# Where in a slot VectorE's side work is issued: an attention and FFN kernel on one core

## Chip, core and metric

The kernel runs on one core of one Trainium2 chip. The metric is the device time of one execution in microseconds (us). The kernel before takes 370.85 us, the median of three runs (370.76 to 371.12). One more execution was recorded with the hardware profiler, and all rows of the profile come from that one.

## What is computed

The inputs are q, k and v with 8 batches, 8 heads, 576 positions and 64 features, s with one value per batch, head and position, and the three weight matrices and the norm vector of an FFN. All are float32.

```python
scores = scale * np.matmul(q, k.transpose(0, 1, 3, 2))
cum = np.cumsum(np.maximum(s, 0.0), axis=-1)
bias = -(cum[:, :, :, None] - cum[:, :, None, :])
scores = np.where(causal, -1e9, scores + np.minimum(bias, 0.0))
attn = softmax(scores)                   # with 1e-9 in the denominator
x = (attn @ v), heads side by side       # 4608 tokens of 512
xn = x / sqrt(mean(x * x) + 1e-6) * rms_g
out = (silu(xn @ w_gate) * (xn @ w_val)) @ w_out
```

## The kernel before

**Two kinds of work in one stream.** The FFN is cut into nine chunks of 512 tokens (chunk 0 starts at 30.9 us, chunk 1 at 72, chunk 2 at 111, chunk 3 at 150, chunk 4 at 190, chunk 5 at 227). The attention of batch 0 runs ahead of chunk 0; that of later batches is threaded through the chunks. A function `ffn` writes a chunk's matmuls: twelve pairs of gate (L670, with wg_sb) and value matmuls (L679, with wv_sb) of four each, and then the out-projection (L692), four blocks of twelve. Their results lie in four PSUM buffers, psF, taken in turn. ScalarE makes a tanh T of the gate (L673), VectorE the product U (L682) and then Ht (L675, L687); U frees the gate's buffer, Ht the other. ScalarE copies a block of the out-projection from its psF to osb (L697), and SyncE sends it out (L699).

**Slots.** Between these matmuls, 36 times per chunk, `ffn` calls `step`. A call is a slot: it writes a few pieces of attention into the engines' queues. Nothing is rescheduled afterwards (the kernel asks for a manual schedule), so the order in which `step` writes is the order in which every engine works. In a slot come, in this order:

1. What is left of the score step begun in the slot before: the second half of its exponentials on ScalarE (L274), and on GpSimd the causal mask over them (L283).
2. x_scale (L338), if a token block's values are three slots old: VectorE multiplies the block by its norm factor al_all and the norm vector. SyncE's transposing DMA (L348, L350) then brings the block into xnT, from which the FFN chunks read.
3. One piece from each of several queues of side work: loads on ScalarE (`act_side`), transposing DMAs for keys and queries (L171), loads of v and k (`v_side`, `pool_side`) and casts on GpSimd.
4. One piece from `dve_side`, VectorE's side work.
5. Either a score step or up to two of: a transposition of the norm's output (`do_xt`), a value step (`do_av`), a transposition of keys or queries (`do_t`). With a score step of batch 1, a `do_t` may come as well.

**Side work of VectorE.** `dve_side` holds two casts of batch 1's Q (L141), and for every batch's keys and queries a range check: `check_mag` strips the signs into mag (L369, 128 x 2560), and two calls of `check_max` take a running maximum into acc (L375, 128 x 1280 each). Nobody reads acc before the end of the kernel. From the third batch on, the checks are issued in the last slots of a chunk, during the out-projection. The end of the kernel adds a few small steps for a range test.

**A score step** (`do_s`, L250) multiplies keys with queries on TensorE into the one score buffer, psS. Four or eight exponentials (L274) read it, half of them in the slot itself, half at the head of the next. The next score step waits until they are done.

**A value step** (`do_av`, L300 and L306) multiplies the exponentials with v for four heads. The result goes to one of two PSUM buffers, psAV for the first half of the heads and psT for the second. VectorE forms a reciprocal of the sums (L313) and multiplies (L315) into x_sb; the text calls this pair the values. Behind the second half, ScalarE squares x_sb with a running sum (L321, the Square), GpSimd makes the norm factor from it (L328, L331), and x_scale of a later slot uses that.

These are the lines in question in the value step:

```python
nc.vector.reciprocal(out=rZ[0:n], in_=pv[0:n, :, 64])
...
nc.vector.tensor_tensor(
    out=xo[:, g * 256:(g + 1) * 256].rearrange("p (h d) -> p h d", h=4),
    in0=pv[0:n, :, 0:64], in1=rZ[0:n].unsqueeze(2).to_broadcast([n, 4, 64]), op=ALU.mult)
```

The slot itself and what calls it:

Of the kernel before, what the change touches and what calls it, by code (L numbers as in the profile page):

```python
# [26 lines left out]
def kernel(  # L27
# [131 lines left out]
    def kq_dma(b, w, c):  # L159

        if w == 0:
            n = rows(c)
            src = kqn[0:n, b % 2, 0, c].rearrange("p h d -> p (h d)")
            dst = kqTx[:, b % 2, 0, c, :, 0:n]
        elif c < 4:
            src = kqn[32 * c:32 * c + 32, b % 2, w, 0:4].rearrange("p r h d -> p (r h d)")
            dst = kqTx[:, b % 2, w, c].rearrange("d h (r p) -> d (h r) p", r=4)
        else:
            src = kqn[0:64, b % 2, w, 4].rearrange("p h d -> p (h d)")
            dst = kqTx[:, b % 2, w, 4, :, 0:64]  # L170
        nc.sync.dma_start_transpose(out=dst, in_=src)  # L171
# [50 lines left out]
    def slot_free():  # L222
        return eread.get(ecount[0] % NE, 0) == 0
# [111 lines left out]
    def x_scale(b, qb):  # L335
        n = rows(qb)
        col = b * NSC + qb
        nc.vector.scalar_tensor_tensor(  # L338
            out=xs_sb[0:n, (b * NSC + qb) % NX, :], in0=x_sb[0:n, (b * NSC + qb) % NX, :],
            scalar=al_all[0:n, col:col + 1], in1=g_row[0:n], op0=ALU.mult, op1=ALU.mult)  # L340

    def xt_dma(b, qb):

        n = rows(qb)
        t0 = (b * S + qb * 128) % RING
        m = min(n, RING - t0)
        i = (b * NSC + qb) % NX
        nc.sync.dma_start_transpose(out=xnT[:, :, t0:t0 + m], in_=xs_sb[0:m, i, :])  # L348
        if m < n:
            nc.sync.dma_start_transpose(out=xnT[:, :, 0:n - m], in_=xs_sb[m:n, i, :])  # L350
# [46 lines left out]
    def at(*key):  # L397
        return done.get(key, 10 ** 6)

    def ready(lag, *key):  # L400
        return at(*key) + lag <= slot[0]

    def run_side(queue):
        if queue and queue[0][0]():
            queue.pop(0)[1]()
            return True
        return False
# [21 lines left out]
    def phase():  # L429

        return slot[0] - first[0]
# [14 lines left out]
    def casts(b):  # L446

        def key(c):  # L450
            load_k(b, c)
            done["K", b, c] = slot[0]
            if c == NSC - 1:
                check(b)

        def over(w):
            done["cast", b, w] = slot[0]
            if b + 1 < B and (w == 1 or b + 1 < KB):
                loads(b + 1, w, early, 4)
            if w == 1:  # L460
                x_seq.extend((b, ww, c) for c in range(NSC) for ww in ((1, 0) if b >= KB else (1,)))
            else:
                done["cast", b] = slot[0]
                check(b)

        def free(w):
            return ready(0, "check", b - 2, w) and (
                ready(0, "T", b - 2) if w == 0 and b < KB + 2 else
                b < XB + 2 or ready(4, "X", b - 2, w, 4))
        if b >= KB:  # L470
            pool_side.extend((lambda: free(0) and slot[0] % 2 == 0, lambda c=c: key(c)) for c in range(NSC))
        fns = [(1, lambda r=r: cast_x(nc.gpsimd, b, 1, r)) for r in range(NSC)]
        fns += [(1, lambda: over(1))]
        if b < KB:
            fns += [(0, lambda r=r: cast(nc.gpsimd, b, 0, r, r + 1)) for r in range(NSC)]
            fns += [(0, lambda: over(0))]
        pool_side.extend((lambda w=w: ready(7, "raw", b, w) and free(w), f) for w, f in fns)
# [11 lines left out]
    def do_t(key, **kw):  # L489
        b, hp, w = key  # L490
        if hp == "tail":
            tail_step(b)
            done["T", b] = slot[0]
            after_tail(b)
        else:
            if b == 1:
                kw["dve"] = w == 1 and hp > 1
                if hp % 2:
                    kw["pT"] = psF16()
            t_step(b, hp, w, **kw)  # L500
        done["T", b, hp, w] = slot[0]
        last["T"] = slot[0]

    def do_s(key, pair=None):
        b, kb, g = key
        second = s_step(b, kb, g, pair)
        done["S", b, kb, g] = slot[0]
        if kb == 4:
            done["S", b, 4, 1] = slot[0]
        last["S"] = slot[0]  # L510
        return second
# [18 lines left out]
    def can_t():  # L530
        if not t_seq:
            return False
        b, hp, w = t_seq[0]
        if b >= XB and at(*(("XT", 1, 3) if b == 2 else ("AV", b - 1, (2, 1, 0, 0, 0)[b - 3], 1))) > slot[0]:
            return False
        if b >= XB and av_seq[0][2] == 1 and can_av(True):
            return False
        if slot[0] - last["T"] < (1 if b < XB else 2 if b < 4 else 3) or slot[0] - last["AVT"] < 3:
            return False
        return (ready(2, "cast", b) or ready(2, "cast", b, w)) and (b < 2 or ready(1, "S", b - 2, 4, 0))  # L540

    def can_s():
        if not s_seq or not slot_free():
            return False
        b, kb, g = s_seq[0]
        if b == 1 and (phase() < 24 and phase() % 2 == 0 or kb == 4 and at("AV", 1, 3, 1) > slot[0]):
            return False
        due = SLOTS * ((b * S + kb * 128) // DM) - (26 if b == 1 else 18 if b < 4 else 14)
        if slot[0] - last["S"] < (4 if slot[0] < due - 24 else 3 if slot[0] < due else 2):
            return False  # L550
        if b >= XB:
            return all(ready(5, "X", b, 1, c) for c in (kb, min(kb + 1, 4))) and (
                ready(5, "X", b, 0, kb) if b >= KB else ready(3, "T", b) if kb >= 3 else
                all(ready(3, "T", b, hp, 0) for hp in (2 * g, 2 * g + 1)))
        if kb >= 3 and not ready(3, "T", b):
            return False
        if kb == 4:
            return True
        return all(ready(3, "T", b, 2 * g + j, w) for j in (0, 1) for w in (0, 1))
# [18 lines left out]
    def by_pe(b, qb):  # L578

        return b == 0 or (b, qb) == (1, 3)  # L580

    def can_xt():
        if not xt_seq or slot[0] - last["T"] < 2:
            return False
        b, qb = xt_seq[0]
        if (b, qb) == (0, 4) and at("T", 1) > slot[0]:
            return False
        return ready(4 if b else 6, "AV", b, qb, 1) and by_pe(b, qb)
# [10 lines left out]
    def step(bare=False):  # L599

        slot[0] += 1
        while pending:
            pending.pop(0)()
        moved = False
        if scaled[0] < len(x_list):
            b, qb = x_list[scaled[0]]
            if ready(3, "AV", b, qb, 1):
                x_scale(b, qb)
                scaled[0] += 1
                if not by_pe(b, qb):  # L610
                    assert xt_seq[0] == (b, qb)
                    xt_dma(*xt_seq.pop(0))
                    done["XT", b, qb] = slot[0] + 4
                    moved = True
        run_side(act_side)

        if not moved and x_seq and slot[0] - last["X"] >= 2 and not (
                scaled[0] < len(x_list) and ready(1, "AV", *x_list[scaled[0]], 1)):
            b, w, c = x_seq[0]
            if (ready(2, "cast", b, 1) and ready(1, "S", b - 2, 4, 0)  # L620
                    and (w == 1 or ready(7, "K", b, c))):
                x_seq.pop(0)
                kq_dma(b, w, c)
                done["X", b, w, c] = last["X"] = slot[0]
                if b >= KB and (w, c) == (0, NSC - 1) and b + 2 < B:
                    casts(b + 2)
        bare = bare or chunk[0] == 0 and 30 <= phase() <= 33
        if slot[0] % 2 and not bare and not (chunk[0] == 0 and phase() >= 24):
            run_side(v_side)
        if not bare:  # L630
            run_side(pool_side)
        run_side(dve_side)
        if can_s():
            pending.append(do_s(s_seq.pop(0)))
            if t_seq and t_seq[0][0] == 1 and can_t():
                do_t(t_seq.pop(0))
            return
        n = 0
        if can_xt():
            do_xt(xt_seq.pop(0))  # L640
            n += 1
        if can_av():
            do_av(av_seq.pop(0))
            n += 1
        if n < 2 and t_seq and can_t():
            do_t(t_seq.pop(0))
# [466 lines left out]
```

## Time and profile before

| | us |
|---|---|
| median of three runs | 370.85 (370.76 to 371.12) |
| the profiled execution | 371.13 |
| its span, first to last instruction | 369.5 |
| TensorE (PE) busy in it | 346.3 |
| VectorE (DVE) busy | 277.1 |
| ScalarE (ACT) busy | 238.4 |
| GpSimd (POOL) busy | 176.1 |
| mean granted TensorE clock | 0.998 |

TensorE's busy time by stage: 19.55 of the 30.9 us ahead of chunk 0, 116.84 of the 119.1 us of chunks 0 to 2, 38.08 of the 40 us from 150 to 190 (chunk 3), 109.21 of the 110 us from 190 to 300, and 62.66 of the last 69.5 us.

How to read the profile: a row of a timeline gives start, length, engine, source line, what is written from what, and in brackets the engine's idle time in front with what ended it. "[0.96 <-ACT E L274]" says that the engine had nothing to do for 0.96 us, until ScalarE's line 274 had written E. Rows that follow each other on one engine overlap by some 0.08 us, because an instruction starts while the one before it drains. PEld is the loading of weights, which runs beside the matmuls. An average share of busy time says little here: what counts is whether TensorE waits, and for whom, in a given stage.

### The profile page before, as it was taken

The page shows a single profiled execution, that of the slowest core. Times are in us where ns is not written, and L with a number is a line of the kernel's source. Part 1 is how long each engine was busy: PE and PEld are TensorE (multiplying, and loading weights), DVE is VectorE, ACT ScalarE, POOL GpSimd, SP SyncE. Part 2 cuts the span into 40 slices and gives each one's busy share as a digit, 9 for nine tenths or more (in the row PEclk, how much of TensorE's full clock was granted, in tenths as well). Part 3 has the DMA queues.
Part 4 walks back from the last instruction along what each step waited for, and adds up shares of the span by engine and source line. Part 5 has one row for each costly group of instructions (what it writes and reads, how often), then busy time and mean ns, then how long its engine had stood idle before and what let it go on. Part 6 is the DMA issues. An engine that isn't in the chain of part 4 may idle for free.

```text
span 369.5 us, 6891 instructions
## 1 busy us (share of the span) xinstructions
PE 346.3 (94%) x2312; PEld 162.7 (44%) x2356; DVE 277.1 (75%) x523; ACT 238.4 (64%) x624; POOL 176.1 (48%) x281
## 2 busy tenths in 40 slices
PE   1888999999999999899999999999999999999992
PEld 1554544444444444444444444444444444444441
DVE  6777989599887878789989889885488558827820
ACT  3977686557896688677678766776677644223311
POOL 4968637948648375779637933632222200000000
PEclk9999999999999999999999999999999999999999
DMA  8999999999969299949969964992300230020011
GB/s 233 172 231 244 165 221 220 157 206 201 181 131 122 44 200 150 170 92 181 146 171 189 167 97 129 107 96 51 106 17 14 44 106 3 0 85 30 0 60 63
DMA packets 125627, 46.23 MB, mean 125 GB/s; under 512 B 104912, under 2 KB 120784, under 8 KB 125584
## 3 DMA queue, kind: packets, MB, share of 16 engines
q0 software_dynamic: 59920, 11.80, 45.5%
q1 hardware_dynamic: 53040, 24.33, 33.4%
q10 hardware_dynamic: 12624, 9.59, 10.6%
q8 instruction: 20, 0.33, 0.4%
q14 instruction: 23, 0.19, 0.2%
HBM read 38.16 MB, written 9.44 MB: 129 GB/s over the span
## 4 chain that ended last, share of the span: by engine, by line
PE 69%; DVE 9%; POOL 7%; issue 5%; DMA 5%; ACT 4%; ACTq 0%; SPq 0%; POOLq 0%; DVEq 0%
PE psF L692 22%; PE psF L670 19%; PE psF L679 19%; PE psS L250 4%; DMA kq<-in_q_dram 3%; ACT E L274 2%; POOL v_sb L175 2%; DVE acc L375 2%; DVE U L682 2%; DVE Ht L675 2%; POOL E L283 2%; DMA kq<-in_k_dram 2%; DVE x_sb L315 1%; POOL kqn L141 1%; PE psT L306 1%
## 5 line engine op out<-in xcount | busy, mean ns | idle before, releaser
L274 ACT ACTIVATE E<-psS,biasK 128x256 bf16<-128x256 f32 (+3 forms) x352 | 114.9, 415 | 19.2 <-PE psS L250 17.8
L670 PE MATMUL psF<-xnT,wg_sb 128*128 128x512 bf16 x426 | 110.2, 379 | 1.3 <-ACT xnT L364 0.7
L679 PE MATMUL psF<-xnT,wv_sb 128*128 128x512 bf16 x408 | 109.3, 379 | 1.3
L692 PE MATMUL psF<-wout_sb,Ht 128*128 128x512 bf16 x419 | 100.5, 379 | 0.5 <-issue 0.2
L682 DVE SCALAR_TENSOR_TENSOR U<-T,psF 128x512 bf16<-128x512 f32 x108 | 73.7, 682 | 29.0 <-ACT T L673 28.9
L283 POOL TENSOR_SCALAR_AFFINE_SELECT E<-E 128x512 bf16<-128x512 bf16 x72 | 52.2, 726 | 83.9 <-ACT E L274 83.5
L673 ACT ACTIVATE T<-psF 128x512 f32<-128x512 f32 x108 | 64.5, 597 | 42.1 <-PE psF L670 36.7
L675 DVE TENSOR_TENSOR Ht<-U,psF 128x512 bf16<-128x512 bf16 x99 | 67.7, 684 | 6.6
L670 PEld LDWEIGHTS <-wg_sb 128*128 128x128 bf16 x432 | 38.8, 98 | 45.7 <-issue 6.6
L679 PEld LDWEIGHTS <-wv_sb 128*128 128x128 bf16 x432 | 38.6, 98 | 42.5 <-issue 4.4
L692 PEld LDWEIGHTS <-Ht 128*128 128x128 bf16 x432 | 38.7, 98 | 42.0 <-issue 2.3
L338 DVE SCALAR_TENSOR_TENSOR xs_sb<-x_sb,al_all,g_row 128x512 bf16<-128x512 bf16 (+1 forms) x40 | 32.1, 804 | 15.0 <-POOL al_all L331 15.0
L697 ACT ACTIVATE osb<-psF 128x512 f32<-128x512 f32 x36 | 21.4, 595 | 31.8 <-PE psF L692 29.0
L321 ACT ACTIVATE xs_sb<-x_sb 128x512 bf16<-128x512 bf16 (+1 forms) x36 | 22.9, 639 | 22.8 <-DVE x_sb L315 22.5
L175 POOL DMA_DIRECT2D v_sb<-in_v_dram x40 | 35.0, 874 | 0.3 <-issue 0.2
L375 DVE TENSOR_TENSOR acc<-acc,mag 128x1280 bf16<-128x1280 bf16 x32 | 29.0, 921 | 0.4
L250 PE MATMUL psS<-kqT 64*128 64x256 bf16 (+2 forms) x304 | 26.8, 262 | 2.6 <-ACT E L274 2.0
L306 PEld LDWEIGHTS <-E 128*128 128x128 bf16 x320 | 23.1, 101 | 11.4 <-POOL E L283 0.8
L328 POOL TENSOR_SCALAR al_all<-ss_all 128x1 f32<-128x1 f32 (+1 forms) x40 | 12.6, 316 | 28.2 <-ACT xs_sb L321 23.7
L300 PEld LDWEIGHTS <-E 128*128 128x128 bf16 x256 | 21.2, 101 | 8.1 <-DVE x_sb L315 0.7
L331 POOL TENSOR_TENSOR al_all<-al_all,mhalf 128x1 f32<-128x1 f32 (+1 forms) x40 | 22.2, 555 | 3.3
L250 PEld LDWEIGHTS <-kqT 64*128 64x128 bf16 x320 | 10.4, 97 | 30.5 <-issue 29.2
(94 smaller groups left out, 280.4 us busy)
## 6 DMA issues: line engine op xcount, KB each, us to landing
out_dram<-osb SPq DMA_DIRECT2D x36, 256.0 KB, 2.2
kq<-in_q_dram ACTq DMA_DIRECT2D x6, 1024.0 KB, 7.8
v_sb<-in_v_dram POOLq DMA_DIRECT2D x32, 128.0 KB, 7.6
kq<-in_k_dram ACTq DMA_DIRECT2D x2, 1024.0 KB, 11.0
kqn<-in_k_dram POOLq DMA_DIRECT2D x16, 128.0 KB, 4.7
wg_sb<-in_moe_w_gate_dram POOLq DMA_DIRECT2D x2, 768.0 KB, 9.4
wv_sb<-in_moe_w_val_dram POOLq DMA_DIRECT2D x2, 768.0 KB, 12.0
wout_sb<-in_moe_w_out_dram POOLq DMA_DIRECT2D x1, 1536.0 KB, 15.0
```

What stands on the lines that cost most here:

```text
L175: nc.gpsimd.dma_start(out=v_sb[0:n, b % 2, c, :, 0:64], in_=v[b, :, c * 128:c * 128 + n, :].rearrange("h p d -> p h d"))
L250: nc.tensor.matmul(pair[par][:, j * W:j * W + M], lhsT=kT, rhs=qT, start=(j == 0), stop=(j == nj - 1))
L274: nc.scalar.activation(out=eo, in_=ei, func=AF.Exp, scale=0.125, bias=biasK[:, kb, bh:bh + 1])
L283: nc.gpsimd.affine_select(out=Ev[:, :, 0:nq], in_=Ev[:, :, 0:nq], pattern=[[0, nh], [1, nq]], compare_op=ALU.is_ge, fill=0.0, base=0, chan ...
L338: nc.vector.scalar_tensor_tensor(out=xs_sb[0:n, (b * NSC + qb) % NX, :], in0=x_sb[0:n, (b * NSC + qb) % NX, :], scalar=al_all[0:n, col:col ...
L375: nc.vector.tensor_tensor(out=acc[:, sl], in0=acc[:, sl], in1=mag[:, sl], op=ALU.max)
L670: nc.tensor.matmul(Gp, lhsT=wg_sb[:, cc, fs], rhs=xnT[:, cc, x0:x0 + DM], start=(cc == 0), stop=(cc == CC - 1))
L673: nc.scalar.activation(out=T, in_=Gp, func=AF.Tanh, scale=0.5)
L675: nc.vector.tensor_tensor(out=Ht[:, fb - 1, :], in0=pend[0], in1=pend[1], op=ALU.mult)
L679: nc.tensor.matmul(Vp, lhsT=wv_sb[:, cc, fs], rhs=xnT[:, cc, x0:x0 + DM], start=(cc == 0), stop=(cc == CC - 1))
L682: nc.vector.scalar_tensor_tensor(out=U, in0=T, scalar=1.0, in1=Gp, op0=ALU.add, op1=ALU.mult)
L692: nc.tensor.matmul(Op, lhsT=Ht[:, fb, tb * 128:(tb + 1) * 128], rhs=wout_sb[:, fb, :], start=(fb == 0), stop=(fb == FB - 1))
```

## The change

The body of the slot behind the call for `dve_side` becomes a function of its own, `place`, and is called ahead of it. So steps 4 and 5 of the list above trade places: in a slot that has both, VectorE gets the instructions of the score, value or transposition step first, and the piece of side work behind them. Which slot a piece falls into doesn't change.

```diff
@@ in step
             run_side(v_side)
         if not bare:
             run_side(pool_side)
+        place()
         run_side(dve_side)
+
+    def place():
+
         if can_s():
             pending.append(do_s(s_seq.pop(0)))
             if t_seq and t_seq[0][0] == 1 and can_t():
```

## The prediction

> **What bounds the kernel.** The busy times come first. TensorE is busy 346.3 of 369.5 us, so the other engines matter only where they make it wait.
>
> ```profile
> PE 346.3 (94%) x2312; PEld 162.7 (44%) x2356; DVE 277.1 (75%) x523; ACT 238.4 (64%) x624; POOL 176.1 (48%) x281
> ```
>
> Next, TensorE's waits. Most of its idle time is the lead-in before the first FFN chunk at 30.9 us and the tail, which the change leaves alone. Behind that, only one group has a size: scores (L250) that wait for ScalarE's exponentials.
>
> ```profile
> PE psS L250 <- ACT E L274: 2.0, 4, 1.0
> ```
>
> TensorE's timeline gives the places. The two largest are the second score step of chunk 3 and the last score step behind that chunk's out-projection. Both wait for the one score buffer (psS), which is free once four exponentials have read it.
>
> ```profile
> 154.08 0.39 PE L250 MATMUL psS<-kqT 64*128 64x256 bf16 x4 [0.96 <-ACT E L274]
> 189.34 0.39 PE L250 MATMUL psS<-kqT 64*128 64x256 bf16 x4 [0.58 <-ACT E L274]
> ```
>
> Why are the exponentials late? ScalarE's timeline: each time a Square (L321) heads its queue and has idled 2.0 and 2.5 us for VectorE's values (x_sb, L315). Behind the Square stand an output copy (L697) and the exponentials, with nothing between them.
>
> ```profile
> 150.88 0.63 ACT L321 ACTIVATE xs_sb<-x_sb 128x512 bf16<-128x512 bf16 x1 [2.00 <-DVE x_sb L315]
> 151.51 0.58 ACT L697 ACTIVATE osb<-psF 128x512 f32<-128x512 f32 x1
> ...
> 153.17 0.86 ACT L274 ACTIVATE E<-psS,biasK 128x256 bf16<-128x256 f32 x2
> ...
> 186.62 0.63 ACT L321 ACTIVATE xs_sb<-x_sb 128x512 bf16<-128x512 bf16 x1 [2.50 <-DVE x_sb L315]
> ```
>
> And why are the values late? VectorE's timeline, two short windows for the first place and a longer one for the second: the reciprocal (L313) that opens the values stands right behind range-check maxima (L375).
>
> ```profile
> 148.28 0.83 DVE L375 TENSOR_TENSOR acc<-acc,mag 128x1280 bf16<-128x1280 bf16 x1
> ...
> 149.02 1.27 DVE L375 TENSOR_TENSOR acc<-acc,mag 128x1280 bf16<-128x1280 bf16 x1
> 150.22 0.17 DVE L313 RECIPROCAL rZ<-psT 128x4 f32<-128x4 f32 x1
> ...
> 184.89 1.15 DVE L375 TENSOR_TENSOR acc<-acc,mag 128x1280 bf16<-128x1280 bf16 x1
> 185.96 0.17 DVE L313 RECIPROCAL rZ<-psT 128x4 f32<-128x4 f32 x1
> ```
>
> The products that these reciprocals read were finished long before: TensorE's last value matmul starts at 148.72 (0.19 long) and at 182.72.
>
> **What moves.** Set side by side, the two programs have the same instructions; the order differs on VectorE only. ScalarE, GpSimd, SyncE with all its DMAs, and TensorE keep theirs. Eleven of VectorE's side instructions trade places: one maximum with a key/query copy in chunk 0, nine maxima and one mask (L369) with a pair of reciprocal and product. The two casts of batch 1's Q don't move: no values stand in their slots. Nothing is added or removed, so the sum is one of waits.
>
> **Does a moved reciprocal block the queue?** It is VectorE's only new risk of waiting, since the maximum would then be stuck behind it. At each place I compared the time at which VectorE would reach the reciprocal with the end of its matmuls: 101.0 against 100.7, 139.5 against 139.2, 149.05 against 148.9, 181.6 against 178.9, 184.9 against 182.9, 189.8 against 187.0, 218.1 against 218.15, 223.1 against 222.3, 224.4 against 224.3, 226.6 against 226.5. At most 0.1 us each: cost 0. In chunk 0 the copy at 45.33 could go at 44.60 and its transposes ended at 43.5; TensorE has no gap there until 53.55 (0.34, behind exponentials of a later score step): 0.
>
> **First place (154.08).** The second maximum goes behind the values, so the reciprocal starts at about 149.05 instead of 150.22: 1.17 earlier. Bounds: 0.8, if the maximum were as short as its neighbour (0.83), and 1.17; I take 1.15, the row itself. The Square goes from 150.88 to 149.73, the copy to 150.36 (its matmuls end at 148.75 + 1.03 = 149.78, so it isn't held), the exponentials to 150.83 (scores ready at 149.71 + 0.39 = 150.10), the tanh to 151.55 (gate matmuls end at 151.15), the last exponentials end at 154.03 - 1.15 = 152.88. TensorE finishes the gate matmuls in front at 152.09 + 1.03 = 153.12. So TensorE, not psS, is late next: the whole 0.96 goes, with 0.24 to spare. **-0.96** (with the short maximum: -0.7).
>
> **Second place (189.34).** Before, the reciprocal of 185.96 stood behind two maxima of this stage, two masks, a pair of values and the third maximum (1.15). After, that third maximum stands behind it: 185.96 - 184.89 = 1.07 earlier. The Square goes to 185.55, the copy to 186.18 (its matmuls end at 182.75 + 2.75 = 185.50), the four exponentials end at 189.29 - 1.07 = 188.22; TensorE is done with the out-projection at 186.87 + 1.89 = 188.76. The 0.58 goes whole, with 0.5 to spare. The chain of waits names matmuls as what released the copy at 187.25; but it starts as the Square's accumulator read does elsewhere (0.09 behind it, no idle time), so I put it down to the Square. If the chain is right, this place gives 0. **-0.58**
>
> **The other places** give the engine behind them time that TensorE doesn't wait for: no gap over 0.17 us stands between 190 us and the end. **0**
>
> **What could be given back.** (a) At 139.56 the maximum now stands in front of x_scale (L338, 141.12): 139.53 + 0.55 of values + 0.75 = 140.85, still before it. But this x_scale leads, through the next values, Square and x_scale at 145.47, to a transposing DMA issued at 146.25; with 3.8 us, the median landing of that stretch, it lands at 150.05, and chunk 3's first matmul is at 150.13. Whatever delays it by over 0.1 us, TensorE pays. The nearest rows are a maximum of 0.83 (gain of up to 0.26, hidden) and one of 1.27 (x_scale 0.2 late). I take 0.1, and keep 0 and 0.2.
>
> A rule bears on this: the Trainium skill, "SBUF — State Buffer", section "Who interferes with whom", says that a VectorE instruction with two SBUF inputs and a GpSimd instruction that reads SBUF exclude each other, and that the one issued first holds the shared port to its end. This trace agrees: GpSimd's 0.19 us row L328 took 0.79 at 139.65, beside a maximum begun 0.09 earlier, and the maximum of 149.02 took 1.27 with a GpSimd select at 148.96 to 149.62. By that rule the moved maximum would stand behind GpSimd's L331, which would run from about 139.9 to 140.5, and end at 141.25; the sum would have 0.13 here in place of 0.1.
>
> (b) The FFN stage runs close: its four psF buffers are freed by VectorE, and at 174.60 the gate matmuls start 0.05 behind the product that freed theirs, at 207.44 the same. TensorE keeps its gain only if VectorE is as much earlier. It is: 1.15 against 0.96, then 1.15 + 1.07 against 1.54. Cost 0; if VectorE kept only 1.15 by 207, TensorE would lose 0.4.
>
> **Sum.** -0.96 - 0.58 + 0.1 = -1.44 us. The profiled execution took 371.13 us, 1.63 outside its span of 369.5; this one would have 368.1 and 369.7. It is 0.28 above the median of 370.85, so I forecast **369.4** as a median (0.39% less).
>
> **Rivals.**
> - Only one place closes. The first alone: 370.85 - 0.96 + 0.1 = 370.0, if the chain of waits is right about 187.25. The second alone: 370.3 to 370.4, if x_scale's lateness (0.2) and a short maximum take the first. For it: both margins rest on starts 0.2 to 0.5 us apart. Against: the links are in-order queues without idle time.
> - Nothing is kept: 370.85. Chunks 3 and 4 are tied to VectorE by (b), and an earlier TensorE only meets later buffers there. For it: DVE is busy 17.03 of the 19.5 us from 154.5 to 174. Against: its idle time there ends with ScalarE's tanh, which comes earlier too.
> - Slower: maxima meet GpSimd. At chunk 4's head two maxima stand together in front of the last values and the first U (L682, 192.69); before they took 1.13 and 0.81. The longest maximum of the trace took 2.27 (86.16, beside two GpSimd casts). Two such cost 4.54 - 1.94 = 2.60 more. The third gate matmuls' weights load 0.54 after that U frees their buffer, so TensorE pays from 0.54 on: 2.06. With the first place gained and the second not, +1.1: 371.95. Against: the median maximum is 0.82, and GpSimd has no cast from 182.1 to 196.
>
> **Chances.** Forecast 0.50; first place alone 0.13, second alone 0.07; nothing 0.17; slower 0.13. About 0.2% (0.74 us) is what a measurement of this kernel can tell from no change. Faster by more: 0.50 + 0.13 = 0.63; within it: 0.07 + 0.17 = 0.24; slower: 0.13. The forecast's own range is 369.0 (TensorE's 0.15 gap at 177.28, before another score step, goes too, and nothing is given back) to 369.8 (0.4 lost by 207). With the single places and with nothing kept it reaches to 370.9, which leaves out the slower case.
>
> **What would show it.** Right: no wait before the scores that stood at 154.08 and 189.34; the Squares' idle times of 2.00 and 2.50 down by about 1.1 each; chunk 3 starting within 0.1 us of 150.1. Wrong: a wait at the same scores with a later Square; a gap before chunk 3's first gate matmul; TensorE waiting for U or Ht at 170 to 210; maxima of over 1.2 us in the new places.

## The result and the profile after

| | before | after |
|---|---|---|
| median, run in turn on one chip, 7 runs each | 370.76 us (369.7 to 371.24) | 368.74 us (368.38 to 370.21) |
| ratio, 95% interval | | 0.9957 (0.9938 to 0.9976) |
| the profiled execution | 371.13 us, span 369.5 | 370.21 us, span 368.6 |

The changed kernel is faster by 0.43% (0.24 to 0.62%), or 1.6 us of 370.76 (0.9 to 2.3). That is the ratio of the means; the medians alone lie 2.0 us apart. The busy times hardly differ, as they should with the same instructions. Of the waits for scores a quarter is left, in chunks 0 and 1. From the page of the changed kernel and its list of waits (total us, number, longest):

```profile
PE 345.4 (94%) x2312; PEld 161.6 (44%) x2356; DVE 278.7 (76%) x523; ACT 239.0 (65%) x624; POOL 174.1 (47%) x281
...
PE psS L250 <- ACT E L274: 0.5, 2, 0.3
```

TensorE's timeline after, at the two places that waited 0.96 and 0.58. There is no bracket any more, so no idle time in front:

```profile
154.39 0.39 PE L250 MATMUL psS<-kqT 64*128 64x256 bf16 x4
188.99 0.39 PE L250 MATMUL psS<-kqT 64*128 64x256 bf16 x4
```

ScalarE's timeline after: the two Squares, whose idle time was 2.00 and 2.50 and is now 0.74 and 0.84.

```profile
150.81 0.63 ACT L321 ACTIVATE xs_sb<-x_sb 128x512 bf16<-128x512 bf16 x1 [0.74 <-DVE x_sb L315]
185.25 0.63 ACT L321 ACTIVATE xs_sb<-x_sb 128x512 bf16<-128x512 bf16 x1 [0.84 <-DVE x_sb L315]
```

VectorE's timeline after, first place: the reciprocal now stands between the two maxima, and idles 0.26 for its matmuls. The second maximum takes 0.82, not 1.27.

```profile
149.05 0.83 DVE L375 TENSOR_TENSOR acc<-acc,mag 128x1280 bf16<-128x1280 bf16 x1
150.14 0.18 DVE L313 RECIPROCAL rZ<-psT 128x4 f32<-128x4 f32 x1 [0.26 <-PE psT L306]
...
150.70 0.82 DVE L375 TENSOR_TENSOR acc<-acc,mag 128x1280 bf16<-128x1280 bf16 x1
```

So two executions can be compared, I measure each chunk from the first weight load of its first gate matmul to that of the next chunk (us):

| profile | to chunk 0 | chunk 0 | 1 | 2 | 3 | 4 |
|---|---|---|---|---|---|---|
| before | 30.00 | 42.12 | 38.99 | 38.98 | 39.56 | 37.36 |
| before, a second profile | 29.84 | 41.54 | 39.00 | 39.21 | 38.89 | 37.37 |
| after | 30.07 | 43.20 | 39.00 | 39.15 | 37.88 | 37.36 |
| after, a second profile | 29.73 | 41.51 | 39.80 | 39.14 | 37.88 | 37.35 |

From chunk 5 on all four agree within 0.01 us, up to the tail. The gain is in chunks 2 and 3: 78.54 and 78.10 before, 77.03 and 77.02 after. Chunks 0 and 1 vary by 1.7 and 0.8 us with the same program, and the tail by 0.6, which is why one profiled execution of the changed kernel is only 0.92 us below that of before. In it chunk 0 met a stretch at half clock (columns: window, length, busy time of PE, PEld, DVE, ACT and POOL, granted clock, DMA share, GB/s):

```profile
31.10:34.50 3.40, 3.18 (x8) 1.22 (x8) 3.40 (x3) 1.64 (x3) 3.19 (x5) 0.50 1.23 241
```

The granted clock is 0.50 for 3.41 us there, and 1.00 in the same stretch of the other three. The comparison below therefore uses chunks 2 and 3 of each profile beside the timed ratio.

### The profile page after: what moved, and what is told of

The parts are those of the page before. It is cut to its first block, busy times and chain, and to the rows that moved or that the text cites. A ratio compares the mean times of both kernels' runs of the same rounds, so it can differ in the third digit from the quotient of the medians.

```text
span 368.6 us, 6892 instructions
## 1 busy us (share of the span) xinstructions
PE 345.4 (94%) x2312; PEld 161.6 (44%) x2356; DVE 278.7 (76%) x523; ACT 239.0 (65%) x624; POOL 174.1 (47%) x281
## 4 chain that ended last, share of the span: by engine, by line
PE 78%; POOL 7%; issue 5%; DVE 4%; ACT 3%; DMA 2%; ACTq 0%; POOLq 0%; DVEq 0%
PE psF L696 25%; PE psF L674 21%; PE psF L683 21%; PE psS L250 5%; ACT E L274 2%; POOL E L283 2%; POOL v_sb L175 2%; DMA kq<-in_k_dram 2%; POOL kqn L141 1%; PE psT L306 1%; PE psAV L306 1%; PE psAV L300 1%; PE psT L300 1%; POOL al_all L331 1%; DVE Ht L679 1%
## 5 line engine op out<-in xcount | busy, mean ns | idle before, releaser
L283 POOL TENSOR_SCALAR_AFFINE_SELECT E<-E 128x512 bf16<-128x512 bf16 x72 | 50.9, 707 | 93.1 <-ACT E L274 92.7
L338 DVE SCALAR_TENSOR_TENSOR xs_sb<-x_sb,al_all,g_row 128x512 bf16<-128x512 bf16 (+1 forms) x40 | 32.1, 803 | 13.9 <-POOL al_all L331 13.9
L321 ACT ACTIVATE xs_sb<-x_sb 128x512 bf16<-128x512 bf16 (+1 forms) x36 | 23.0, 640 | 16.2 <-DVE x_sb L315 16.1
L306 PEld LDWEIGHTS <-E 128*128 128x128 bf16 x320 | 22.4, 99 | 12.2 <-POOL E L283 1.9
L331 POOL TENSOR_TENSOR al_all<-al_all,mhalf 128x1 f32<-128x1 f32 (+1 forms) x40 | 23.7, 593 | 3.3
L300 PEld LDWEIGHTS <-E 128*128 128x128 bf16 x256 | 20.6, 99 | 8.2 <-DVE x_sb L315 1.0
L328 POOL TENSOR_SCALAR al_all<-ss_all 128x1 f32<-128x1 f32 (+1 forms) x40 | 10.4, 260 | 24.0 <-ACT xs_sb L321 18.0
```

The lines of the kernel that those rows point to most:

```text
L283: nc.gpsimd.affine_select(out=Ev[:, :, 0:nq], in_=Ev[:, :, 0:nq], pattern=[[0, nh], [1, nq]], compare_op=ALU.is_ge, fill=0.0, base=0, chan ...
L306: nc.tensor.matmul(o, lhsT=d, rhs=v_sb[:, p, qb, h, :], start=(j == 0 and qb == 0), stop=(j == 3))
L338: nc.vector.scalar_tensor_tensor(out=xs_sb[0:n, (b * NSC + qb) % NX, :], in0=x_sb[0:n, (b * NSC + qb) % NX, :], scalar=al_all[0:n, col:col ...
```

## The experiments

My theory after the result was that of the prediction: a Square without its values holds ScalarE's queue, and each place is closed by its own trade, the first by the one in slot 35 of chunk 2, the second by those of chunk 3. Rivals: only one of them counts; the amount of VectorE's work counts and not its place; the wait moves elsewhere.

The kernels that do a part of the change alone all have this body of the slot, with a different CONDITION:

```diff
-        run_side(dve_side)
+        late = CONDITION
+        if not late:
+            run_side(dve_side)
+        place()
+        if late:
+            run_side(dve_side)
```

All results but e8's, which has its own paragraph, in one table. The waits are those of TensorE in that run's profile, under 0.1 us shown as a dash; "2 + 3" is the length of chunks 2 and 3.

| run | chunk 3's start | its second score step | its last score step | 2 + 3 | time against before (95%) |
|---|---|---|---|---|---|
| before | - | 0.96 | 0.58 | 78.54 | |
| before_again | 0.25 | 0.75 | - | 78.10 | |
| after | 0.18 | - | - | 77.03 | 0.9957 (0.9938 to 0.9976) |
| e7, after again | 0.18 | - | - | 77.02 | 0.9983 (0.9957 to 1.0010) |
| e1, slot 35 of chunk 2 | 0.20 | - | 0.58 | 77.70 | 0.9983 (0.9967 to 0.9998) |
| e2, chunk 3 | 0.27 | 0.74 | - | 77.95 | 1.0009 (0.9988 to 1.0030) |
| e3, all others | 0.37 | - | - | 77.37 | 0.9988 (0.9976 to 1.0001) |
| e4, Squares on VectorE | 0.90 | - | - | 77.76 | 0.9977 (0.9954 to 1.0000) |
| e5, one maximum more, before | 0.23 | 1.63 | 0.10 | 78.98 | 1.0024 (1.0015 to 1.0034) |
| e6, one maximum more, after | 0.26 | - | - | 77.10 | 0.9956 (0.9941 to 0.9970) |
| e10, slot 26 of chunk 2 | - | 0.19 | - | 77.25 | 0.9963 (0.9934 to 0.9991) |
| e11, all but slot 26 | - | - | - | 76.94 | 0.9958 (0.9939 to 0.9977) |
| e9, second maximum later | - | 0.22 | - | 77.09 | 0.9958 (0.9934 to 0.9981) |

In every row 2 + 3 is 76.9 plus the row's waits, within 0.2 us. Two things have to be kept in mind. A late start of the chunk is hidden by a wait behind it: before loses 0.96 at the second score step, its second profile 0.25 and 0.75, e2 0.27 and 0.74, about 1.0 each time. And the timed ratios are too coarse to rank the versions (e3 and e10 differ by 0.25% with intervals that overlap), so the argument rests on the profiles, of which most versions have one.

### The parts of the change (e1, e2, e3)

e1: CONDITION is `(chunk[0], phase()) == (2, 35)`. e2: `chunk[0] == 3`. e3: `chunk[0] != 3 and (chunk[0], phase()) != (2, 35)`.

> Only the last swap of chunk 2 is made (the maximum of 149.02 goes behind the values); everything else is as before. Queue theory (the values stand behind the maximum, the Square and the exponentials behind the values, the scores behind the exponentials): the wait of 0.96 us in front of the second score step of chunk 3 is gone, the wait of 0.58 us at the end of chunk 3 stays; chunk 3 goes from 39.56 to about 38.6 us and the time by -0.9 us (369.8 where before has 370.76). Rival (the gain comes from the other swaps, or from somewhere else in the program): under 0.3 us.

> Only the three swaps at the end of chunk 3 are made. Queue theory (the output copy of 187.25 stood behind a late Square): the wait of 0.58 us at the end of chunk 3 is gone, the wait of 0.96 us stays; chunk 3 goes from 39.56 to about 39.0 us, the time by -0.55 us (370.2). Rival (the chain of waits is right that the copy was released by its matmuls): the Square comes 1.1 us earlier, the wait of 0.58 us stays, 0 us.

> All swaps but those of the two runs above: the one of chunk 0, the one of chunk 1, the first of chunk 2 and the four of chunk 4. Queue theory: both waits stay at 0.96 and 0.58 us, chunks 1, 2 and 4 keep 39.0, 39.0 and 37.4 us within 0.2 us, 0 us in time. Rival (the measured 2.0 us are more than the 1.44 forecast because these swaps bring something too): -0.5 us, to be found in chunk 0 or at the end.

e1 and e2 look as the theory wants: each takes away its own wait and leaves the other. e3, which should have left both, has neither (its start waits 0.37, which can hide as much at the second score step). So the theory of one trade for one wait fell, and with it the reading of e2: a wait that can be gone without the trade isn't shown to be closed by it.

### Is it the Square at the head of ScalarE's queue? (e4)

Tile (3,3) is batch 3's block 3 of 128 positions, counted from 0. In the order of before, the Squares of tiles (3,3) and (4,3) go to VectorE (L325 takes the place of L321):

```diff
-        act = act or b > 1 or b == 1 and qb > 1
+        act = act or (b > 1 or b == 1 and qb > 1) and (b, qb) not in ((3, 3), (4, 3))
```

> The order is that of before; only the Squares behind those two late values are done by VectorE instead of ScalarE (its form of batch 0, about 0.7 to 1.0 us), so that ScalarE's output copy and exponentials no longer stand behind them. The values stay as late as before. Queue theory (what costs the time is that the Square heads ScalarE's queue): both waits are gone, chunk 3 goes from 39.56 to about 38.0 us, the time by -1.4 us (369.3). Rival (the late values themselves, or VectorE's load, hold TensorE by another way, such as x_scale or U): both waits stay and VectorE's 0.7 us more add to it, 0 to +0.7 us; by the chain of waits the first is gone and the second stays, -0.9 us.

VectorE's and ScalarE's timelines of e4. The maxima take 2.02 and the reciprocal is as late as before. But ScalarE's copy and exponentials no longer stand behind a Square: the copy starts 0.37 ahead of the reciprocal.

```profile
148.51 2.02 DVE L375 TENSOR_TENSOR acc<-acc,mag 128x1280 bf16<-128x1280 bf16 x2
150.46 0.17 DVE L313 RECIPROCAL rZ<-psT 128x4 f32<-128x4 f32 x1
```

```profile
150.09 0.60 ACT L697 ACTIVATE osb<-psF 128x512 f32<-128x512 f32 x1 [0.97 <-ACT E L274]
150.58 0.83 ACT L274 ACTIVATE E<-psS,biasK 128x256 bf16<-128x256 f32 x2
152.28 0.60 ACT L673 ACTIVATE T<-psF 128x512 f32<-128x512 f32 x1 [0.87 <-PE psF L670]
```

The wait of 0.96 is gone with late values. But chunk 3's start waits 0.90 here (the last experiment's subject), and that alone would hide most of 0.96. The last row settles it: ScalarE is through with the first exponentials and idles 0.87 for the late gate matmuls, so it, and not TensorE, is ahead. Without the late start the exponentials would end, by an estimate from these rows, some 41.4 us after chunk 2's start (111.33 in e4), and TensorE comes to its second score step at 42.0 in before. So late values cost TensorE time only through the Square in ScalarE's queue, and that link of the prediction holds. The timed ratio ends at 1.0000 and settles nothing.

### Place or amount? (e5, e6)

One more maximum in slot 35 of chunk 2: in e5 in front of the values (order of before), in e6 behind them (order of after).

```diff
+        if (chunk[0], phase()) == (2, 35):
+            check_max(1)
```

> Before, with one more maximum (0.82 us, the second half of the same mask once more) in the slot of the last value step of chunk 2, at the head of the slot as all side work there. Queue theory: these values, their Square, the copy and the exponentials come 0.8 us later; the waits at chunk 3's start and before its second score step add up to about 1.8 us instead of 1.0, chunks 2 and 3 together take about 79.3 us instead of 78.5, the time rises by 0.8 us over before. Rival (a maximum on VectorE costs nothing by its place, the gain came from elsewhere): 0 us.

> After, with the same additional maximum in the same slot, which there stands behind the values. Queue theory: VectorE has 1.7 us without work there, so nothing waits for it: chunks 2 and 3 as in after (77.0 us, at most 0.2 more), 0 us against after. Rival (it is VectorE's load that counts, not the place): +0.8 us against after.

VectorE's row and the score row of e5: three maxima in front of the reciprocal, and a wait of 1.63.

```profile
147.87 2.88 DVE L375 TENSOR_TENSOR acc<-acc,mag 128x1280 bf16<-128x1280 bf16 x3
150.67 0.18 DVE L313 RECIPROCAL rZ<-psT 128x4 f32<-128x4 f32 x1
```

```profile
154.54 0.40 PE L250 MATMUL psS<-kqT 64*128 64x256 bf16 x4 [1.63 <-ACT E L274]
```

VectorE of e6: the same maximum behind the values, and no wait at a score step of chunk 3.

```profile
150.38 0.18 DVE L313 RECIPROCAL rZ<-psT 128x4 f32<-128x4 f32 x1 [0.27 <-PE psT L306]
...
150.94 1.68 DVE L375 TENSOR_TENSOR acc<-acc,mag 128x1280 bf16<-128x1280 bf16 x2
```

A maximum of 0.83 in front takes the waits at chunk 3's start and second score step together from 0.96 and 1.00, in the two profiles of before, to 1.86: 0.86 to 0.90 us more, and 0.9 us (0.24% of 370) in time. Behind, it costs 0.07 us in chunks 2 and 3, and the ratio is that of the changed kernel. Place decides, not amount.

### The changed kernel again, and a failed improvement (e7, e8)

e7 is the changed kernel, unedited. e8 removes the maximum that stands in front of the second half of tile (3,2): it notes the end of a check together with the second maximum, one slot earlier, and skips three slots in chunk 2.

```diff
+            if chunk[0] == 2 and phase() in (27, 28, 30):
+                return False
...
+        def last_max(w):
+            check_max(1)
+            done["check", b, w] = slot[0]
...
-            lambda w=w: check_mag(b, w), lambda: check_max(0), lambda: check_max(1),
-            lambda w=w: done.__setitem__(("check", b, w), slot[0])))
+            lambda w=w: check_mag(b, w), lambda: check_max(0), lambda w=w: last_max(w)))
```

> The changed kernel once more, on the same chip and beside the same runs of before as the others. Queue theory with what the first runs showed (chunk 3's start waits 0 to 0.4 us for a transposing DMA, whatever the order): -1.4 us with a spread of half a microsecond, chunk 2 and 3 together about 77.0 us against 78.0 to 78.5. Rival (the 2.0 us measured first are the change's own): -2.0 us, with a shorter stretch outside chunks 2 and 3.

> After, and two things more: the entry that only notes that a check is finished is joined to its second maximum (a check takes three slots instead of four), and in chunk 2 no side work is issued in the slots 27, 28 and 30, so that no maximum stands in front of the values of the block whose transposing DMA chunk 3's start waits for, and only one piece runs while GpSimd makes that block's norm factor. In chunk 1 the range checks of batch 1 then end before the slot in which a maximum took 2.27 us beside GpSimd's casts. Queue theory: chunk 3's first block is transposed about 0.6 us earlier, its start no longer waits (0.2 us), and the wait of 0.38 us for U in chunk 1 is gone: -0.5 us against after, about -1.9 against before. Rival (that DMA's landing is set by the DMA queues, not by its issue): chunk 3's start waits as before, -0.3 us against after.

e7 repeats the profile of after in chunks 2 and 3 (77.02); its times scatter from 368.16 to 372.75, and its ratio, 0.17% faster with an interval that reaches 0.10% slower, can't tell a gain from none by itself. e8 is slower: 1.0162 (1.0135 to 1.0190). Its list of waits (its lines behind the slot stand 8 further down: L678 is the gate matmul L670, L690 the U of L682):

```profile
ACT xs_sb L321 <- DVE x_sb L315: 26.5, 21, 3.6
...
PE psS L250 <- ACT E L274: 3.5, 6, 2.4
...
PE psF L678 <- DVE U L690: 2.0, 2, 1.2
```

The noted end of a check is also what lets GpSimd's casts, and behind them loads and transposing DMAs, be issued. With it one slot earlier and three slots skipped, GpSimd, ScalarE and VectorE work in another order, and chunks 2 and 3 took 82.5 us; e8 doesn't separate the two edits. It says nothing about the maximum; e9 repeats the question without this side effect.

### Which trade does it? (e10, e11)

In e3, the trade in slot 26 of chunk 2 had the first half of tile (3,2) ahead of a maximum. e10 does this trade alone, `(chunk[0], phase()) == (2, 26)`; e11 all but this one, with `!=`. A second profile of before went with them.

> The kernel before, with only the trade in slot 26 of chunk 2 (values of tile (3,2), first half, ahead of a maximum). Theory now: this one trade, which the prediction put at 0 gain, brings the x_scale of (3,2) about 0.4 us earlier and moves the second maximum of slot 35 away from GpSimd's mask, so that it takes about 0.82 us instead of 1.27, and most of the 0.96 us wait before the second score step of chunk 3 goes without the trade in slot 35; the wait of the last score step (0.58) stays or shrinks by luck. Chunks 2 and 3 together then take 77.8 to 78.2 us against 78.5 of the kernel before, the time is 0.3 to 0.7 us less. Rival: that the run of all other trades closed the wait was chance; then 78.4 to 78.6 us and no change in the time.

> The changed kernel without the trade in slot 26 of chunk 2. Theory: the two score waits are closed by the trades in slot 35 of chunk 2 and in chunk 3, so both stay away; chunk 3's start is released by the landing of a transposing DMA and not by the x_scale; chunks 2 and 3 take 77.0 to 77.3 us as in the changed kernel. Rival: the trade in slot 26 is what pays in chunk 2; then chunk 3's start waits 0.4 us or more longer than the 0.18 of the changed kernel and the two chunks take 77.5 us or more.

> A second profile of the kernel before, to see how much of its waits is chance from one execution to the next. The second score step of chunk 3 waits 0.8 to 1.1 us and its last score step 0.5 to 0.6, chunks 2 and 3 take 78.3 to 78.7 us; if one of the waits is missing here, single profiles can't be used to tell the trades apart.

e10, with one trade for which the prediction had written 0, gets most of the gain: chunks 2 and 3 take 77.25, under the 77.8 to 78.2 that I expected (the last score step doesn't wait here, a matter of chance, as the next part shows), against 78.10 in the second profile of before, which doesn't wait there either, and 77.03 after.

What it changes first stands at the traded maximum. GpSimd's step of the norm factor (L328) and x_scale (L338), in the first profile of before and then in e10:

```profile
139.65 0.79 POOL L328 TENSOR_SCALAR al_all<-ss_all 128x1 f32<-128x1 f32 x1 [1.22 <-ACT xs_sb L321]
141.12 0.75 DVE L338 SCALAR_TENSOR_TENSOR xs_sb<-x_sb,al_all,g_row 128x512 bf16<-128x512 bf16 x1 [0.18 <-POOL al_all L331]
```

```profile
140.21 0.19 POOL L328 TENSOR_SCALAR al_all<-ss_all 128x1 f32<-128x1 f32 x1 [1.23 <-ACT xs_sb L321]
141.29 0.75 DVE L338 SCALAR_TENSOR_TENSOR xs_sb<-x_sb,al_all,g_row 128x512 bf16<-128x512 bf16 x1
```

In before the maximum starts just ahead of L328, which then takes 0.79, and x_scale idles until the factor is there. In e10 the values stand at that place instead, the maximum comes later, L328 takes 0.19, and x_scale comes 0.37 earlier against chunk 2's start, which is at 111.11 in before and 111.66 in e10.

The timelines of VectorE and GpSimd in e10, then of the second profile of before, at the two maxima in front of the reciprocal:

```profile
148.43 1.56 DVE L375 TENSOR_TENSOR acc<-acc,mag 128x1280 bf16<-128x1280 bf16 x2
...
149.53 0.98 POOL L283 TENSOR_SCALAR_AFFINE_SELECT E<-E 128x512 bf16<-128x512 bf16 x1 [0.65 <-ACT E L274]
```

```profile
147.56 2.02 DVE L375 TENSOR_TENSOR acc<-acc,mag 128x1280 bf16<-128x1280 bf16 x2
...
148.25 0.66 POOL L283 TENSOR_SCALAR_AFFINE_SELECT E<-E 128x512 bf16<-128x512 bf16 x1 [0.24 <-ACT E L274]
```

The earlier x_scale brings what stands behind it on VectorE forward, through the next values, Square and x_scale, by 0.41 us at the second maximum (37.51 after chunk 2's start, not 37.92). That puts it 0.36 ahead of GpSimd's mask instead of 0.05 behind it. Now the mask waits (0.98) and not the maximum: 1.56 for two instead of 2.02. The two effects, 0.41 and 0.46, make the reciprocal 0.87 earlier against its chunk, and the wait falls to 0.19. e11, without this trade, has no wait either. The first place can be closed twice over; the change does both, and the second closing has nothing left to gain.

### One wait that was chance

The second profile of before is the same program, and its last score step doesn't wait. VectorE's and GpSimd's rows in the first profile and in the second, shortly ahead of the maxima of the second place:

```profile
178.14 1.71 POOL L149 CAST kqn<-kq 128x512 bf16<-128x512 f32 x3
179.16 1.23 DVE L338 SCALAR_TENSOR_TENSOR xs_sb<-x_sb,al_all,g_row 128x512 bf16<-128x512 bf16 x1
```

```profile
177.44 2.24 POOL L149 CAST kqn<-kq 128x512 bf16<-128x512 f32 x3
178.46 0.75 DVE L338 SCALAR_TENSOR_TENSOR xs_sb<-x_sb,al_all,g_row 128x512 bf16<-128x512 bf16 x1
```

In both, x_scale starts 1.02 after the first of three casts, and the third cast 0.08 to 0.09 after x_scale. In the first profile x_scale is 0.48 longer; in the second the casts are 0.53 longer. One of the two stands until the other is through, and the rows don't tell which: in the profile of after the third cast is 0.08 behind too, as in before, and x_scale takes 0.75. Of the 13 profiles but e8's, x_scale lost in two, before and e1. Those are just the two with the wait of 0.58. Everything behind x_scale follows it: ScalarE's copy at 187.25 comes 37.15 after chunk 3's start in the first profile and 36.47 in the second (186.07), 0.09 behind the Square's accumulator read in each. Of these 0.68, 0.48 are x_scale's and 0.2 the longer wait at the second score step.

The place costs something even when x_scale wins. I compare the weight loads of chunk 3 with those of the profile of after: behind its second score step chunk 3 loses 0.65 in the first profile of before and 0.64 in e1. In the four profiles without the trades of chunk 3 in which x_scale won (the second of before, e3, e5 and e10; e4, whose Squares are moved, apart) it still loses 0.16 to 0.20 there, and nothing in the others with these trades (e7, e2, e6, e9 and e11).

### What sets chunk 3's start? (e9)

e9 has the second maximum of every check one slot later, in the slot in which the end of the check is noted; the queues of GpSimd, ScalarE and SyncE keep their order.

```diff
-            lambda w=w: check_mag(b, w), lambda: check_max(0), lambda: check_max(1),
-            lambda w=w: done.__setitem__(("check", b, w), slot[0])))
+            lambda w=w: check_mag(b, w), lambda: check_max(0), lambda: None,
+            lambda w=w: (check_max(1), done.__setitem__(("check", b, w), slot[0]))))
```

> The changed kernel, with the second maximum of every check one slot later (in the slot in which the end of the check is noted, so that GpSimd's casts and the loads keep their slots). No maximum stands then right ahead of the second half of tile (3,2). If chunk 3's start is set by VectorE, its x_scale comes 0.4 us or more earlier, chunk 3's wait of 0.18 at its start goes, and chunks 2 and 3 take 76.8 us or less. If the transposing DMA's own queue sets the landing, x_scale comes earlier and the landing doesn't: 77.0 us, as in the changed kernel. Either way the waits of the second score step of chunk 3 and of its last one stay away, and the time is within 0.3 us of the changed kernel's.

In all 13 profiles chunk 3's first weights are loaded behind the landing of the transposing DMA that brings tile (3,2), in 11 of them 0.06 us behind it (in the other two, e9 and e10, it landed in time and TensorE didn't wait). Of before and then of after, the last two DMAs issued up to and with this one (us from issue to landing last):

```profile
kqn<-in_k_dram POOLq DMA_DIRECT2D x1, 128.0 KB, 4.2
xnT<-xs_sb SPq DMA_TRANSPOSE x1, 3.8
```

```profile
kqn<-in_k_dram POOLq DMA_DIRECT2D x1, 128.0 KB, 4.8
xnT<-xs_sb SPq DMA_TRANSPOSE x1, 4.3
```

After issues it 34.75 us behind chunk 2's start, before 35.13; yet it lands at 39.09 against 38.92. A load of k from GpSimd, issued 0.6 to 0.9 us ahead of it, lands 0.2 to 0.35 ahead of it in both. The five profiles with the slot 26 trade and the old places of the maxima (after, e3, e6, e7, e10) issue it 0.4 us earlier than the others, and it lands hardly earlier (38.77 to 39.27, median 39.09; the others without e9 38.92 to 39.81, median 39.14). e9 issued at 35.18, late, and landed at 38.31, with the load at 38.06. So x_scale's time didn't set chunk 3's start in these runs. That the load holds the DMA up is argued from the order of landings; no run took the load away, and it stays open.

e9's x_scale of (3,2) came at 34.40, against 33.97 after: I expected 0.4 us earlier and it was 0.4 later, since GpSimd's step of the norm factor ahead of it (L328) was caught beside a mask strip on VectorE and took 0.64 instead of 0.20. Chunks 2 and 3 took 77.09, as in the changed kernel. Chunk 1 took 38.34 instead of 39.00 (the wait of 0.38 at its ninth gate matmuls is gone), but the timed ratio is the same 0.9958: no version here beats the changed kernel by what the runs can tell.

## Why the prediction was right, point by point

The forecast was 369.4 against 370.85, 0.39% less; measured were 0.43% less (0.24 to 0.62%), and 0.17% (-0.10 to 0.43%) when the same kernel was timed again as e7. By the ratio, 370.85 becomes 369.26, inside the forecast's range of 369.0 to 369.8; the median itself, 368.74, lies under it. Direction and place (chunks 2 and 3) were right, and so was the chain of waits; that the size came out so near is partly luck, since the second of its two terms hangs on a tie that x_scale lost in two of 13 profiles. Of the terms:

- **First place, -0.96.** Right. The wait, 0.96 and 0.75 in two profiles of before, is gone in both of after, and e4 and e5 show the chain from reciprocal over Square to exponentials. The reciprocal came 1.24 earlier against chunk 2's start, where 1.15 to 1.17 was forecast. What the step missed is that the wait had two independent cures. (The alternative with a short maximum was off by its own rows: exponentials 0.8 earlier give 0.8, not 0.7.)
- **Second place, -0.58.** The mechanism was right, the term was mis-sized: it was read from one execution in which x_scale had lost a tie. It lost that tie in two of the 13 profiles; a typical execution of before had only 0.2 to lose there, as the second profile, e3, e5 and e10 show. The doubt about the chain of waits (matmuls as the releaser of the copy at 187.25) is answered: the copy moved with the Square. No run shows the trades of chunk 3 together with an x_scale that lost. An estimate says that they would have closed the wait: the Square comes 33.82 after chunk 3's start in after, with them, and 35.00 in e3, without, which is 1.18 earlier, and the lost tie delays it by 0.48 (35.48 in e1).
- **The other places, 0.** Wrong as a reason. The prediction quoted the row of L328 that took 0.79 beside the maximum of slot 26, but looked for gaps of TensorE behind each traded slot and called an earlier x_scale hidden. It didn't follow it along VectorE's queue: 0.41 us on, it changed who collided with whom, worth 0.77 of the first 0.96.
- **Give-back (a), +0.1.** Measured: chunk 3's start waits 0.18 after, against none and 0.25 before. The size was near, but the reason failed. VectorE's and GpSimd's rows after, at the moved maximum:

```profile
141.10 0.56 POOL L331 TENSOR_TENSOR al_all<-al_all,mhalf 128x1 f32<-128x1 f32 x1
141.18 0.81 DVE L375 TENSOR_TENSOR acc<-acc,mag 128x1280 bf16<-128x1280 bf16 x1
141.92 0.74 DVE L338 SCALAR_TENSOR_TENSOR xs_sb<-x_sb,al_all,g_row 128x512 bf16<-128x512 bf16 x1
```

  L328 in front of L331 took 0.19 instead of 0.79. The maximum starts 0.08 behind L331 and takes 0.81: it isn't held, and x_scale comes 0.36 earlier (29.64 against 30.00 from chunk 2's start), not 0.1 later. What the Trainium skill says in "SBUF — State Buffer", section "Who interferes with whom", that the instruction issued first holds the port to its end, would have held it to the end of that row, 141.66. Here the measurement decides against that reading: as the rows go, the hold was shorter. (By its own numbers the prediction's 140.85 is 140.83, and nothing hangs on it.) The 0.18 is now paid because no wait behind it hides a late start any more.
- **Give-back (b), 0.** Right: no wait for U or Ht appears at 170 to 210, and chunk 4 is 37.36 in both.
- **Blocked reciprocals, 0.** Nearly: the reciprocal of 150.14 idles 0.26 for its matmuls, where I allowed 0.1. ScalarE still has the Square in time.
- **Sum.** -0.96 - 0.58 + 0.1 = -1.44 stood against the profiled execution of before. Between profiles, chunks 2 and 3 give 77.03 - 78.54 = -1.51 with the first and 77.03 - 78.10 = -1.07 with the second. The weight loads divide it up: the start of chunk 3 +0.17 and -0.06, its second score step -1.03 and -0.82, its last one -0.65 and -0.18. With one outcome of the tie in most executions, about -1.1 is what the mechanism explains; that lies within the measured 0.9 to 2.3. The rest of the 1.6, if it is real, isn't assigned. The lower end of the range, 369.0, counted on a gap of 0.15 at 177.28: after has it too (177.58), and the four profiles that record all 2356 matmuls instead of 2312 don't, so it says nothing of the time.

Of the rivals, "nothing is kept" and "slower" found nothing: chunks 4 to 7 keep their lengths, and the two maxima at chunk 4's head took 0.80 and 0.81. Two of the signs of being wrong did appear, at little cost: the gap of 0.18 in front of chunk 3, and a moved maximum of 1.26 (181.81), behind which TensorE shows no wait. "Only one place closes" comes nearest for a typical execution, though not for the reason given.

## What to carry to other kernels

In in-order queues, put work that nobody waits for behind the piece that somebody does, and judge a trade by what stands behind it along its whole queue, not by the gap next to it. Before a wait of half a microsecond enters a sum, look in a second profile whether it is there. A flag that marks the end of a step is part of the schedule too: e8, which moved one by a slot and skipped three slots, lost 1.6%.

## What the runs showed of the hardware

- Which of two engines loses a close collision can't be read from the starts: x_scale took 1.23 with GpSimd's third cast 0.08 behind it (before, e1) and 0.75 with the same 0.08 (after); it lost in 2 of 13 profiles.
- As the rows go, a hold is shorter than the row (GpSimd's rows are rough). In before a mask begun 0.05 ahead of a maximum lengthens it by 0.46, not by the remaining 0.60; after, one begun 0.54 ahead (row 0.66 long) doesn't lengthen it. Taking away the usual length of the one caught, it was free 0.14 to 0.16 before the other's row ended in four pairs: mask and maximum (before), maximum and L328 (before), maximum and mask (e10), maximum and L331 (after).
- The same transposing DMA took 3.1 to 4.6 us to land in 13 profiles, and an issue 0.4 us earlier landed hardly earlier.
- The granted clock fell to 0.50 for 3.41 us at the start of chunk 0 in one profile of the changed kernel, and chunk 0 took 43.20, against 41.51 in the second; the difference arose within its first two pairs. The length of the chunk alone doesn't show this: it took 43.40 in e6 at full clock, with a wait of 1.15 for Ht. The Trainium skill, "TensorE: Matmul & The Clock Gate", section "What's actually happening", gives 3413 ns as the gate's window; the 3.41 us agree.
